# The end of a decode step of two attention and two gated blocks: head 5 with V held still, heads 6 and 7 past the row sum, x laid in rows ahead of them, and a last norm that takes both sums at once

## Chip, cores, metric

One of the eight cores of a Trainium2 chip. The metric is the device time of one execution in microseconds (us). Lower is better. TensorE is PE (its weight loads PEld), VectorE DVE, ScalarE ACT, GpSimd POOL, SyncE SP.

## What is computed

Four tokens (B = 4, one position each, D = 512) go through attention, a gated block, attention and a gated block again, with the same weights and the same cache both times:

```python
x = A_x
x = x + _A_ref(_layernorm(x), A_k_cache, A_v_cache, A_wq, A_wo)
x = x + _B_ref(_layernorm(x), B_w_gate, B_w_up, B_w_down)
x = x + _A_ref(_layernorm(x), A_k_cache, A_v_cache, A_wq, A_wo)
x = x + _B_ref(_layernorm(x), B_w_gate, B_w_up, B_w_down)

# _A_ref: 32 query heads on 8 key/value heads, the last 2048 positions of the cache
p = softmax((x @ wq) @ k^T * 128 ** -0.5);  return (p @ v) @ wo
# _B_ref: F = 1792
return (sigmoid(x @ w_gate) * (x @ w_up)) @ w_down
# _layernorm: (x - mean) / sqrt(var + 1e-5)
```

## The kernel before

Every step is an operation with an engine, a guessed duration, what it reads and writes and a priority (`_Plan.op`, L55). `_schedule` (L96) simulates the engines with these durations and writes down one order for each engine, in which the chip then runs it; a wait is put ahead of an operation for what it reads, for what it overwrites, and for a PSUM bank that another engine used before (`banks`). SP's operations are DMA issues, kept in the order of the program. An engine takes its operations strictly in that order, so an operation that waits holds all that stand behind it.

The first attention (L = 0) and the first gated block (glu 1) are not touched by the change, but for guessed durations. The second attention (L = 2) finds all of K transposed in SBUF (`kt`), so only V is streamed: head by head (`HEADS2`, 0 to 7) into places of `WHERE["V2_h"]`; from head 2 on into the part of `kt` whose head has had its scores. Head 5 has one transfer of 2 MB, head 6 two halves, head 7 one of 1 MB, one of 640 KB and a piece of 384 KB kept from the first attention. Behind V come w_gate, w_up (half of each is kept) and w_down in four pieces for the last gated block.

For a head h (n-th in order; here n = h) of the second attention:

- `scores` (L750): 16 matmuls (L759) into PSUM bank 3 or 0, the maximum on DVE (smax L768, sadd L772, strn L774, smin L778), the exponential on ACT (L781), its transpose on DVE (ptr, L787), and PT, two matmuls (L792);
- `weights` (L804): the probabilities are spread over the four tokens by DVE (ptx, L817) and ACT (pta, L824, four instructions); the row sum zb (L832) and its reciprocal rz (L836). These are the softmax's row sums;
- `pv_wo` (L874): probabilities times V. For heads 2 to 5 (`WIDE[2]`) the probabilities are held still and V moves (`wide_pv`, L852, 32 matmuls of 256 columns); ACT copies the result (L860), and PVs adds its parts up with two float32 matmuls (L867). For the others V is held still (L895, 64 matmuls of 32 columns, in order of the pieces) and nothing is left to add. Then omul (L906, times the reciprocal), a selection by four matmuls (sel, L932), osel (L939), and WO, four matmuls of 512 columns into bank 7 (`WB`, L947), which keeps a sum over heads 0 to 6 (`NWR = 7`) in rows. Head 7 goes past that sum: sixteen matmuls of four columns with wo held still (L917), and the result is added to x directly.

`early_residual(2)` (L954) is planned ahead of head 7: it takes the row sum of bank 7 as a high and a low half (w_hi on ACT, L960, with a load of the sigmoid's table; w_lo on DVE, L966), turns it by eight matmuls (w_turn, L973) and adds it to x (L979).

The last gated block (`glu(3, True)`, L1033) begins with `layer_norm(3)` (L575): xn = x in bfloat16 (L560), x itself (L563), x split into three bfloat16 parts (L583, L585, L586, and x_1 on POOL, L1018), the sum over D by three matmuls (L591) and a reduce (L597), center (L606), square (L618), reduce (L621), a second sum (L579), the variance (L626) and the power -1/2 on POOL (rstd, L630). Beside it the gate and up matmuls run on x not yet normalized (L1050, 112 of four columns), and the mean's part is taken off later (L569, L1066 gc and uc) and rstd multiplied in (L1066 gm and sr). The sigmoid is on ACT (L1071), the product h on DVE (L1090). `x_rows` (L1017) lays x as rows into bank 2 by twelve matmuls (L1026), on which w_down (L1119, 56 matmuls) adds up, so that one copy (L1132) and one DMA write the result.

Of the kernel before, what the change touches and what calls it, by code (L numbers as in the profile page):

```python
# [268 lines left out]
def build(nc, A_x, A_k, A_v, A_wq, A_wo, B_wg, B_wu, B_wd, out):  # L269
# [35 lines left out]
    AHEAD = 2  # L305
    NWR = 7
    WIDE = {0: {0: 4, 1: 4, 2: 4, 3: 4, 4: 4, 5: 4, 6: 2}, 2: {2: 2, 3: 2, 4: 2, 5: 2}}
    VKEEP = {0: 24, 7: 26}
# [30 lines left out]
    with es:  # L339
# [6 lines left out]
        side = nc.alloc_sbuf_tensor_at("side", [128, NS * UNIT], BF16, offset=SIDE)  # L346
        csum = nc.alloc_sbuf_tensor_at("csum", [128, HQ + 2 * NFC], F32, offset=SCRATCH)
        cs_q, cs_g, cs_u = csum[:, 0:HQ], csum[:, HQ:HQ + NFC], csum[:, HQ + NFC:HQ + 2 * NFC]
        ident_r = sb("ident_r", [128, 4 * 128], BF16)
        ident_b = ident_r[:, 0:128]  # L350
# [16 lines left out]
        eye32 = pt[:, 256:288]  # L367
        small = pt[:, 0:1024]
        perm = sb("perm", [128, 128], BF16)
        ofb, ofr = (lambda t: (t[:, 0:NB], t[:, NB:2 * NB]))(sb("ofbr", [128, 2 * NB], F32))  # L370
# [74 lines left out]
        })  # L445
        for h in range(2, HKV - 2):
            WHERE["V2_%d" % h] = [("kt", (h - 2) * UHEAD, UHEAD)]

        def bankb(b):
# [116 lines left out]
        def means(L, out, cs, n):  # L566

            P.op("vector", "mean%d_%d" % (L, n), c_dve(n * NB),
                 lambda v: v.scalar_tensor_tensor(  # L569
                     out[:, :].rearrange("p (f b) -> p f b", b=NB), lr1[:, :].unsqueeze(1).broadcast_to([128, n, NB]),  # L570
                     1.0 / D, cs.unsqueeze(2).broadcast_to([128, n, NB]), ALU.mult, ALU.mult),
                 r=[("pss",), ("cs",)], w=[("mc", id(out))])
            return ("mc", id(out))

        def layer_norm(L, factor=1.0):  # L575
# [5 lines left out]
            if late:  # L581
# [7 lines left out]
                def e_xsum(t):  # L589
                    for i, part in enumerate([by2(xnv)] + x_at[L][1:]):  # L590
# [6 lines left out]
                     lambda v: v.tensor_reduce(lr1[:, :], ps[:, MB, 0:NX].rearrange("p (c b) -> p b c", c=NC), AXX, ALU.add),  # L597
                     r=[("psx",)], w=[("pss",)], banks=(MB,))
            else:
                P.op("vector", "ln_r1_%d" % L, c_dve(NX),  # L600
# [238 lines left out]
        def wide_pv(L, n, h, wide, bank, out, s):  # L839
# [24 lines left out]
            def e_sum(pe):  # L864
                last = None
                for c in range(wide):
# [5 lines left out]
                 w=[("pso", out[0], 0)], banks=(out[0],))  # L872

        def pv_wo(L, n, h, pbk, pieces, prev=()):  # L874
            k2 = n % 2
            kp, ptv, pk = pt_of(L, n)
            wide = WIDE[L].get(n, 0)
            obk = (3 if n == HKV - 1 else pbk[k2]) if L else 6 if wide else 5
            p0 = 0 if L == 0 else 256
# [4 lines left out]
            for s, j0 in () if wide else pieces:  # L884
                def e_pv(pe, s=s, j0=j0):
                    last = None
                    j1 = j0 + s[2] * UNIT // 128
                    for j in range(j0, j1):
# [14 lines left out]
            ov = onb[:, k2 * NR:(k2 + 1) * NR]  # L903
            r0 = p0 if wide else NR
            P.op("vector", "omul%d_%d" % (L, h), c_dve(NR),
                 lambda v: v.tensor_tensor(ov.rearrange("p (r b) -> p b r", r=REP),  # L906
                                           ps[:, obk, r0:r0 + NR].rearrange("p (b r) -> p b r", b=NB),
                                           rz[:, kp * NR:(kp + 1) * NR].rearrange("p (b r) -> p b r", b=NB), ALU.mult),
                 r=[("pso", obk, j0) for _, j0 in pieces] + [("rz", kp)], w=[("on", k2)], banks=(obk,))

            o0 = p0 + 4 * NR if wide else 4 * NR
            if n >= NWR:
                def e_wo(pe):
                    last = None
                    for c in range(NC):
                        for r_ in range(REP):
                            last = pe.matmul(ps[:, obk, o0 + c * NB:o0 + (c + 1) * NB],  # L917
                                             dcol(wo_sb, c, h * WOH + r_ * D),
                                             ov[:, r_ * NB:(r_ + 1) * NB],
                                             start=(c == 0 and r_ == 0), stop=(r_ == REP - 1), skip_group_check=True)  # L920
                    return last
                P.op("tensor", "WO%d_%d" % (L, h), tm["pe_pair"] * NC * REP, e_wo,
                     r=[("wo", h), ("on", k2)], w=[("psl", obk)], banks=(obk,))
                residual("w_acc%d_%d" % (L, h), ps[:, obk, o0:o0 + NX], [("psl", obk)], obk, L == 2 and n == HKV - 1)
                return
# [3 lines left out]
            def e_sel(pe):  # L929
                last = None  # L930
                for j in range(4):
# [9 lines left out]
                                           ofr[:, :].unsqueeze(1).unsqueeze(3).broadcast_to([128, 4, REP, NB]), ALU.mult),  # L941
                 r=[("psl", obk), ("ofr",)], w=[("onr",)], banks=(obk,))

            def e_wo(pe):
                last = None
                for j in range(4):
                    last = pe.matmul(ps[32 * j:32 * j + NR, WB, 0:D], onr[:, j * NR:(j + 1) * NR],  # L947
                                     wo_sb[:, h * WOH + j * D:h * WOH + (j + 1) * D],
                                     start=(n == 0), stop=(n == NWR - 1), skip_group_check=True)
                return last  # L950
# [3 lines left out]
        def early_residual(L):  # L954


            hi, lo = pb[:, 0:D], pb[:, D:2 * D]
            tk = [("psw", n) for n in range(NWR)]
            def e_hi(a):
# [21 lines left out]

        GB, UB, YB = 0, 1, 2
        STASH = ((8, 3), (12, 0), (16, 1), (20, 2))
# [32 lines left out]

        def x_rows():  # L1017
            P.op("gpsimd", "x_1", 300.0, lambda g: g.tensor_copy(x_at[3][0], by2(xnv)), r=[("xn",), ("xz",)], w=[("x1",)])  # L1018

            def e_x(pe):  # L1020
                last = None
                for part in range(3):
                    for i in range(2):
                        for half in range(2):
                            a0 = 32 * (1 - half) + 2 * part + i
                            last = pe.matmul(ps[:, YB, i:128:2], xz[:, a0:a0 + 128], ident_b[:, 64 * half:64 * half + 64],  # L1026
                                             start=(part + i + half == 0), stop=False, skip_group_check=True)
                return last
            P.op("tensor", "x_rows", 12 * tm["pe_pair"], e_x, r=[("x1",), ("x2",), ("x3",), ("ident_b",)],
                 w=[("psyx",)], banks=(YB,), prio=len(P.ops) + 400)  # L1030
            return [("psyx",)]

        def glu(L, last_layer):  # L1033
            GB, UB, YB = (0, 1, 2) if last_layer else (QB, QB + 1, MB)
            layer_norm(L)
            prev = []
            toks = {"g": [], "u": []}
            xin = x_rows() if last_layer else []
            wid = NB if last_layer else NB + 1
            for nm, ktc in (("u", 0), ("u", 1), ("g", 0), ("g", 1), ("g", 2), ("g", 3), ("u", 2), ("u", 3)):  # L1040
# [4 lines left out]
                def e_g(pe, ktc=ktc, s=s, bank=bank):  # L1045
                    last = None
                    for fc in range(NFC):
# [7 lines left out]
                    return last  # L1055
                prev = [P.op("tensor", "glu_%s%d_%d" % (nm, L, ktc), tm["pe_pair"] * NFC, e_g,
                             r=list(blk_tok(s)) + [("xn",)], w=[("psg", bank, ktc)], banks=(bank,), order=prev)]
                toks[nm].append(("psg", bank, ktc))
            NH_ = NFC * NB

# [14 lines left out]
            if last_layer:  # L1075
                mg, mu = means(L, tg, cs_g, NFC), means(L, tu, cs_u, NFC)
                mul("glu_gc", tg, fb(pg), fb(tg), toks["g"] + [mg], mg, (GB,), ALU.subtract)
                mul("glu_gm", gm, fb(tg), rs3, [mg, ("rstd",)], ("gm",))
                P.op("scalar", "glu_sig%d" % L, c_act(NH_), e_sig, r=[("gm",)], w=[("sg",)])
                mul("glu_sr", sg, fb(sg), rs3, [("sg",), ("rstd",)], ("sg",))  # L1080
                mul("glu_uc", um, fb(pu), fb(tu), toks["u"] + [mu], ("um",), (UB,), ALU.subtract)
            else:
                mul("glu_gm", gm, fb(pg), rs3, toks["g"] + [("rstd",)], ("gm",), (GB,))
# [45 lines left out]
            if not last_layer:  # L1129
                residual("glu_res%d" % L, ps[:, YB, 0:NX], ytoks, YB, True)  # L1130
                return
            P.op("vector", "out_cp", c_dve(128), lambda v: v.tensor_copy(pb[:, 0:128], ps[:, YB, 0:128]),  # L1132
                 r=ytoks, w=[("pb", 0)], banks=(YB,))
            dma("out", out_d.rearrange("b (c d) -> c b d", c=NC), pb[0:128:8, 0:128], w=[("out_dram",)], r=[("pb", 0)],
# [27 lines left out]
        def load_wo(h):  # L1162
            to = wo_sb[:, h * WOH:(h + 1) * WOH]
            if h >= NWR:
                dma("wo_%d" % h, to.rearrange("p (r n) -> p r n", r=REP), wo_d[:, h * REP:(h + 1) * REP, :],
                    w=[("wo", h)], rate="bw_1k")
            else:
                dma("wo_%d" % h, to, A_wo[h * REP * 128:(h + 1) * REP * 128, :].rearrange("(p j) n -> p (j n)", j=4),
                    w=[("wo", h)])
# [55 lines left out]
        def v2_head(n):  # L1225
            h = HEADS2[n]
            if n == min(WIDE[2], default=-1):
                eyes(2, sx(20, 1), sorted(set(WIDE[2].values())))
            if n == NWR:
                early_residual(2)  # L1230
            pv_wo(2, n, h, (5, 6), vs2[h], turns[n + 1:n + 2])

# [74 lines left out]
```

## Time and profile before

| what | us |
|---|---|
| median of 3 runs | 175.23 (175.01 to 175.37) |
| the profiled execution | 176.48 |
| its span, first to last instruction | 174.6 (174.64) |
| PE busy | 139.6 (80%) |
| DVE busy | 99.5 (57%) |
| ACT busy | 75.4 (43%) |
| POOL busy | 6.8 (4%) |
| read from HBM | 69.08 MB, 396 GB/s over the span |

The profiled execution is 1.25 us longer than the median; 1.84 us of it lie outside of the span. In the page, a slice is one fortieth of the span (4.37 us), a digit the busy share in tenths, and PEclk the granted clock of TensorE. In the chain of waits each row is a start, a duration and what the end waited for in that stretch: an engine with a tile and a line, a transfer, or "issue" where the profile shows no wait. In the timeline a row is start, duration, engine, line, operation and shapes, and in brackets the idle time ahead of it and what ended that. A matmul's "start to start" is the distance of two such starts in one group; a transfer's landing is its issue plus the time to landing that the trace gives.

### The profile page before, as it was taken

Reading aid. Unit: us, or ns where it says so; the run is one execution under the profiler, and the core shown is the slowest. Engines: PE = TensorE matmul, PEld = TensorE weight load, DVE = VectorE, ACT = ScalarE, POOL = GpSimd, SP = SyncE. Lnnn points to the kernel's source line nnn. Section 1 sums busy time; section 2 is a strip of 40 time slices with the busy share of each in tenths; the row PEclk is TensorE's granted clock in tenths of the full one; section 3 lists DMA queues with packets and bytes.
Section 4 is the critical chain, followed back from the end, with each engine's and each line's share of the span. In section 5 each row is a group of like instructions: output and inputs, shape, how many; then the busy total and the mean of one; then the engine's idle time right before and its main releaser. Section 6 shows DMA issues by size and latency. Waiting matters only on the chain.

```text
span 174.6 us, 4868 instructions
## 1 busy us (share of the span) xinstructions
PE 139.6 (80%) x2175; PEld 102.3 (59%) x2175; DVE 99.5 (57%) x246; ACT 75.4 (43%) x129; POOL 6.8 (4%) x17
## 2 busy tenths in 40 slices
PE   0395589899899679998969776548887999798794
PEld 0293488657566468564745466547424765576693
DVE  7435015886858484795897733014267988842440
ACT  2064216748476636566391240304424654730300
POOL 5200000000000000000000000100100000000020
PEclk9999755999999987999999755555555999955555
DMA  5999999999999999999999999999999999999940
GB/s 181 420 444 408 420 439 424 428 411 443 428 415 426 406 438 424 410 451 409 439 422 401 390 417 416 409 402 394 410 427 436 433 420 418 417 412 424 407 171 5
DMA packets 9504, 69.39 MB, mean 397 GB/s; under 512 B 1032, under 2 KB 2188, under 8 KB 6156
## 3 DMA queue, kind: packets, MB, share of 16 engines
q1 hardware_dynamic: 9476, 69.08, 95.3%
q8 instruction: 17, 0.28, 0.6%
q14 instruction: 3, 0.02, 0.0%
q10 hardware_dynamic: 8, 0.00, 0.0%
HBM read 69.08 MB, written 0.00 MB: 396 GB/s over the span
## 4 chain that ended last, share of the span: by engine, by line
DMA 54%; PE 33%; DVE 5%; ACT 4%; SPq 1%; issue 1%; DVEq 0%; ACTq 0%
DMA arena<-in_A_v_cache_dram 31%; DMA kt<-in_A_k_cache_dram 12%; PE ps L852 7%; PE ps L759 7%; DMA wo_sb<-in_B_w_gate_dram 6%; DMA wo_sb<-in_A_wq_dram 5%; PE ps L736 4%; PE ps L1050 3%; PE ps L895 3%; PE ps L867 2%; SPq L461 1%; PE ps L832 1%; PE ps L947 1%; ACT pb L781 1%; ACT pt L824 1%
## 5 line engine op out<-in xcount | busy, mean ns | idle before, releaser
L746 ACT COPY kt<-ps 128x1024 bf16<-128x1024 bf16 x40 | 39.3, 1016 | 28.9 <-PE ps L736 28.6
L736 PE MATMUL ps<-ident_r,kt 128*128 128x128 bf16 x512 | 40.6, 240 | 5.4 <-DMA kt<-in_A_k_cache_dram 3.2
L736 PEld LDWEIGHTS ps<-ident_r,kt 128*128 128x128 bf16 x512 | 35.3, 111 | 12.1 <-issue 4.0
L746 DVE COPY kt<-ps 128x1024 bf16<-128x1024 bf16 x24 | 29.1, 1214 | 15.1 <-PE ps L736 14.9
L759 PE MATMUL ps<-kt,qs 128*32 128x512 bf16 x256 | 20.4, 448 | 1.3 <-DVE qs L715 0.7
L817 DVE TENSOR_TENSOR pt<-ps,ofbr 128x1024 bf16<-128x1024 f32 (+1 forms) x15 | 15.4, 1030 | 2.7 <-PE ps L792 2.6
L852 PE MATMUL ps<-arena,pt 128*64 128x512 bf16 (+1 forms) x128 | 12.7, 361 | 3.1 <-DMA arena<-in_A_v_cache_dram 3.1
L768 DVE TENSOR_REDUCE nmz<-ps 128x1 f32<-128x512 f32 x16 | 11.0, 687 | 6.8 <-PE ps L759 6.5
L781 ACT ACTIVATE pb<-ps,nmz 128x512 bf16<-128x512 f32 x16 | 11.1, 695 | 5.7 <-DVE nmz L778 5.7
L787 DVE STREAM_TRANSPOSE pb<-pb 128x512 bf16<-128x512 bf16 x16 | 11.2, 702 | 3.8 <-ACT pb L781 3.8
L824 ACT ACTIVATE pt<-ps,ofbr 128x96 bf16<-128x96 f32 x28 | 7.2, 342 | 10.6 <-PE ps L792 10.6
L759 PEld LDWEIGHTS ps<-kt,qs 128*32 128x32 bf16 x256 | 5.9, 105 | 8.3 <-issue 2.6
L852 PEld LDWEIGHTS ps<-arena,pt 128*64 128x64 bf16 (+1 forms) x128 | 5.7, 106 | 7.9 <-DMA arena<-in_A_v_cache_dram 4.0
L832 PE MATMUL ps<-rowf,nmz 128*128 128x16 f32 x32 | 7.3, 304 | 2.3 <-DVE pt L817 2.2
L860 ACT COPY arena<-ps 128x512 f32<-128x512 f32 (+1 forms) x7 | 3.9, 555 | 11.6 <-PE ps L852 11.5
L832 PEld LDWEIGHTS ps<-rowf,nmz 128*128 128x128 f32 x32 | 5.7, 225 | 5.2 <-DVE pt L817 3.5
L630 POOL TENSOR_TENSOR rs<-pt,rs 128x4 f32<-128x4 f32 x4 | 4.1, 1013 | 119.8 <-DVE pt L626 119.8
L867 PEld LDWEIGHTS ps<-arena 128*128 128x128 f32 x52 | 6.7, 201 | 2.1 <-ACT arena L860 1.6
L867 PE MATMUL ps<-arena 128*128 128x16 f32 x52 | 7.4, 273 | 0.7
L1050 PE MATMUL ps<-xn,arena 128*128 128x5 bf16 (+1 forms) x168 | 6.3, 172 | 2.0 <-DMA arena<-in_B_w_up_dram 1.1
L1050 PEld LDWEIGHTS ps<-xn,arena 128*128 128x128 bf16 x168 | 6.3, 118 | 2.2 <-DMA arena<-in_B_w_up_dram 1.2
L947 PE MATMUL ps<-wo_sb,onr 128*16 128x512 bf16 x56 | 6.4, 442 | 1.4 <-DVE onr L939 1.4
(143 smaller groups left out, 158.0 us busy)
## 6 DMA issues: line engine op xcount, KB each, us to landing
kt<-in_A_k_cache_dram SPq DMA_DIRECT2D x8, 2048.0 KB, 24.8
arena<-in_A_v_cache_dram SPq DMA_DIRECT2D x7, 2048.0 KB, 20.1
kt<-in_A_v_cache_dram SPq DMA_DIRECT2D x4, 2048.0 KB, 15.6
wo_sb<-in_A_wo_dram SPq DMA_DIRECT2D x8, 512.0 KB, 25.4
kt<-in_A_v_cache_dram SPq DMA_DIRECT2D x3, 1024.0 KB, 17.0
kt<-in_A_wq_dram SPq DMA_DIRECT2D x1, 2048.0 KB, 11.8
side<-in_A_wq_dram SPq DMA_DIRECT2D x1, 1984.0 KB, 15.9
arena<-in_B_w_up_dram SPq DMA_DIRECT2D x2, 896.0 KB, 8.4
```

Of the source, the lines that this page charges most:

```text
L736: last = pe.transpose(bankb(bank)[:, (v * NB + q) * 128:(v * NB + q + 1) * 128], kt[:, c0:c0 + 128], ident_b[:, :])
L746: return (e.tensor_copy if ev == "vector" else e.copy)(to, fr)
L759: last = pe.matmul(ps[32 * b:32 * b + 32, sbk, 0:CB * 128], qs[:, q0:q0 + 32], blk_ap(kblk(h, b))[:, c * CB * 128:(c + 1) * CB * 128], sta ...
L768: lambda v: v.tensor_reduce(nmv, ps[:, sbk, 0:CB * 128], AXX, ALU.max, negate=True),
L781: o = a.activation(pbuf[:, :], ps[:, sbk, 0:CB * 128], ACTF.Exp, bias=gv, scale=1.0, accum_out=zv)
L787: P.op("vector", "ptr%d_%d" % (L, h), 650.0, lambda v: v.transpose(turned[:, :], pbuf[:, :]), r=[("pb", 0), ("pb", 1)], w=[("pb", 2), ("pb ...
L817: lambda v: v.tensor_tensor(pv4[:, 0:nj], spread(tbk, nj).unsqueeze(2).broadcast_to([128, nj, NB, REP]), ofb[:, :].unsqueeze(1).unsqueeze( ...
L824: last = a.mul(pv4[:, nj:NJ4, b, :], spread(MB, NJ4 - nj), ofb[:, b:b + 1])
L832: lambda pe: pe.matmul(ps[:, tbk, CB * NQ:CB * NQ + NR], zv.broadcast_to([128, 128]), rowf[:, :], start=True, stop=True),
L852: last = pe.matmul(ps[rows * g:rows * (g + 1), bank, 0:wide * 128].rearrange("p (c d) -> p c d", c=wide), ptv[:, w0:w0 + rows], v, start=( ...
L867: last = pe.matmul(ps[:, out[0], out[1]:out[1] + NR], part[:, c * 128:(c + 1) * 128], ey[wide][:, c * NR:(c + 1) * NR], start=(c == 0), st ...
L1050: last = pe.matmul(ps[:, bank, fc * wid:(fc + 1) * wid], cols[:, fc - g0, :], xn[:, ktc * (NB + 1):ktc * (NB + 1) + wid], start=(ktc == 0 ...
```

## The change

- V of head 5 comes in two halves into the same place, and head 5 leaves `WIDE[2]`: V is held still, 64 matmuls of 32 columns.
- `NWR` is by layer: the row sum of the second attention holds heads 0 to 5. Heads 6 and 7 go past it (`wo_last`): wo held still, into bank 5, where the two add up. Head 6 still takes sel and osel, for its wo is laid out for them, and then `oc`, a reduce over the selections.
- `early_residual(2)` is planned ahead of head 6. Its row sum, and later the wo products of heads 6 and 7, are also added as rows to the result (`early_shift`, `wo_rows`; WOr_e, WOr_6, WOr_7, 25x128 matmuls).
- `x_rows` becomes `early_rows`, planned ahead of head 6, with x as it was before the second attention: three groups of four matmuls, and its four steps (x_1, x_rest, x_2, x_3) on POOL. The result's bank YB is 3 instead of 2.
- The last norm (`last_norm`) sums x minus the mean that x had before the second attention (kept by POOL's `s_keep`, taken off by `x_s`) and its square in one reduce and one float32 matmul; variance and mean come out of both sums by five small DVE steps. rstd is multiplied into gate and into up (gm, ur), and no longer into the sigmoid's result.
- gate/up matmuls are planned with 36 ns instead of 29, which moved nothing outside of the end.

```diff
-    NWR = 7
-    WIDE = {0: {0: 4, 1: 4, 2: 4, 3: 4, 4: 4, 5: 4, 6: 2}, 2: {2: 2, 3: 2, 4: 2, 5: 2}}
+    NWR = {0: HKV - 1, 2: HKV - 2}
+    WIDE = {0: {0: 4, 1: 4, 2: 4, 3: 4, 4: 4, 5: 4, 6: 2}, 2: {2: 2, 3: 2, 4: 2}}
...
+        WHERE["V2_%d" % (HKV - 3)] = [("kt", 3 * UHEAD, UHEAD // 2), ("kt", 3 * UHEAD + UHEAD // 2, UHEAD // 2)]
...
+                P.op("gpsimd", "s_keep", 300.0, lambda g: g.tensor_copy(sD, lr1[:, :]), r=[("pss",)], w=[("sD",)])
...
+        GB, UB, YB = 0, 1, 3
+        XB, X0 = 5, 128
+        xsrc = ps[:, XB, X0:X0 + NX]
...
+        def wo_last(n, h):
+            o_ = oc(n)
+
+            def e_wo(pe):
+                last = None
+                for c in range(NC):
+                    for j in range(REP):
+                        last = pe.matmul(ps[:, XB, X0 + c * NB:X0 + (c + 1) * NB], dcol(wo_sb, c, h * WOH + j * D),
+                                         o_[:, j:j + 25:8], start=(n == NWR[2] and c == 0 and j == 0),
+                                         stop=(n == HKV - 1 and j == REP - 1), skip_group_check=True)
+                return last
+
+            P.op("tensor", "WO2_%d" % h, 600.0, e_wo, r=[("wo", h), ("oc", n)], w=[("psl", XB, n)], banks=(XB,))
+            if n < HKV - 1:
+                wo_rows(n, h)
+
+        def wo_rows(n, h, behind=()):
+            o_ = oc(n)
+
+            def e_rows(pe):
+                last = None
+                for j in range(REP):
+                    for c in range(NC):
+                        w0 = h * WOH + j * D + c * 128
+                        last = pe.matmul(ps[32 * c:32 * c + 25, YB, 0:128], o_[:, j:j + 25], wo_sb[:, w0:w0 + 128],
+                                         start=False, stop=False, skip_group_check=True)
+                return last
+            P.op("tensor", "WOr_%d" % h, 600.0, e_rows, r=[("wo", h), ("oc", n), ("psyx",)], w=[("psyr", n)], banks=(YB,),
+                 prio=len(P.ops) + 400, order=behind)
...
+            tail = L == 2 and n >= NWR[2]
+            final = tail and n == HKV - 1
+            to = oc(n).rearrange("p (b y) -> p b y", y=8)[:, :, 0:REP] if final else ov.rearrange("p (r b) -> p b r", r=REP)
...
+            if tail:
+                def e_oc(v):
+                    with nc.allow_low_precision("three of four are zero"):
+                        return v.tensor_reduce(oc(n).rearrange("p (b y) -> p y b", y=8)[:, 0:4],
+                                               onr[:, :].rearrange("p (j r b) -> p j b r", r=REP, b=NB), AXX, ALU.add)
+                P.op("vector", "oc%d_%d" % (L, h), c_dve(4 * NR), e_oc, r=[("onr",), ("xz",)], w=[("oc", n)])
+                wo_last(n, h)
+                return
...
-        def x_rows():
-            P.op("gpsimd", "x_1", 300.0, lambda g: g.tensor_copy(x_at[3][0], by2(xnv)), r=[("xn",), ("xz",)], w=[("x1",)])
...
+        def early_shift():
+
+            P.op("vector", "x_s", c_dve(NX),
+                 lambda v: v.scalar_tensor_tensor(
+                     xs.rearrange("p (c b) -> p c b", c=NC), sD.unsqueeze(1).broadcast_to([128, NC, NB]), -1.0 / D,
+                     xT[:, :].rearrange("p (c b) -> p c b", c=NC), ALU.mult, ALU.add),
+                 r=[("sD",), ("xT",)], w=[("tin",)])
...
+            P.op("tensor", "WOr_e", 320.0, e_h, r=[("pb", u) for u in range(4)] + [("o8",), ("psyx",)], w=[("psyr", 0)], banks=(YB,),
+                 prio=len(P.ops) + 100)
+
+        def early_rows():
+
+            xf, rest = (a.rearrange("p (k i b) -> p k i b", k=2, i=2) for a in (xT[:, :], xr3))
+            x1, x2, x3 = x_at[3]
+            P.op("gpsimd", "x_1", 300.0, lambda g: g.tensor_copy(x1, xf), r=[("xT",), ("xz",)], w=[("x1",)])
+            P.op("gpsimd", "x_rest", 300.0, lambda g: g.tensor_tensor(rest, xf, x1, ALU.subtract), r=[("xT",), ("x1",)],
+                 w=[("xr3",)])
+            P.op("gpsimd", "x_2", 300.0, lambda g: g.tensor_copy(x2, rest), r=[("xr3",), ("xz",)], w=[("x2",)])
+            P.op("gpsimd", "x_3", 300.0, lambda g: g.tensor_tensor(x3, rest, x2, ALU.subtract), r=[("xr3",), ("x2",)], w=[("x3",)])
+            for part in range(3):
...
+                P.op("tensor", "x_rows%d" % part, 480.0, e_x, r=[("x1",), ("x2",), ("x3",), ("ident_b",)] + [("psyx",)] * (part > 0),
+                     w=[("psyx",)], banks=(YB,))
+
+        def last_norm():
...
+            P.op("vector", "xb_last", c_dve(NX), lambda v: v.tensor_tensor(xnv, c4(xsrc), c4(xT[:, :]), ALU.add),
+                 r=toks + [("xT",)], w=[("xn",)], banks=(XB,))
+            P.op("vector", "ln_center3", c_dve(NX), lambda v: v.tensor_tensor(xc[:, :], xsrc, xs, ALU.add),
+                 r=toks + [("tin",)], w=[("xc",)], banks=(XB,))
...
+            P.op("vector", "ln_r12_3", c_dve(2 * NX), lambda v: v.tensor_reduce(part, both, AXX, ALU.add),
+                 r=[("xc",), ("sq",)], w=[("lr2",)])
+            P.op("tensor", "ln_sum3", tm["pe_f32"],
...
+            P.op("vector", "ln_m1", c_dve(NB), lambda v: v.tensor_copy(lr1[:, :], s1), r=[("psv",)], w=[("lr1",)], banks=(MB,))
+            P.op("vector", "ln_m2", c_dve(NB), lambda v: v.scalar_tensor_tensor(m2, lr1[:, :], -1.0 / D, s1, ALU.mult, ALU.mult),
+                 r=[("psv",), ("lr1",)], w=[("lr2",)], banks=(MB,))
+            P.op("vector", "ln_v3", c_dve(NB), lambda v: v.tensor_tensor(m2, s2, m2, ALU.add),
+                 r=[("psv",), ("lr2",)], w=[("lr2",)], banks=(MB,))
...
+            if last_layer:
+                wo_rows(HKV - 1, HEADS2[-1], prev)
...
+                P.op("vector", "glu_ur%d" % L, c_dve(NH_),
+                     lambda v: v.scalar_tensor_tensor(fb(um), fb(um), root, rs3, ALU.mult, ALU.mult),
+                     r=[("um",), ("rstd",)], w=[("um",)])
...
-            if n == NWR:
+            if n == NWR[2]:
+                early_rows()
                 early_residual(2)
+                early_shift()
```

The order that the planner writes for PE around the change, behind the row sum that starts at 150.41 before: x_rows (first four), PT 6, sum of head 4, first half of V5, selection 4, row sum 6, second half of V5, WO 4, PT 7, selection 5, x_rows (eight more), WO 5, row sum 7, first half of V6, kept piece of V7, w_turn, second half of V6, WOr_e, selection 6, wo of head 6, first part of V7, WOr 6, the rest of V7, wo of head 7, 28 gate/up matmuls, ln_sum, 84 gate/up matmuls, WOr 7, w_down.

## Prediction

> **What bounds the kernel now.** I read the granted clock and slices of the page first, then the chain of waits from the second attention on, then the timeline of each engine after 146 us, the landing of each transfer, and the DMA share in short windows near the end.
>
> The page says that DMA is busy to the 38th slice, and that the TensorE clock in the tail is half:
>
> ```profile
> PEclk9999755999999987999999755555555999955555
> DMA  5999999999999999999999999999999999999940
> ```
>
> Windows of 0.5 us (PE, PEld, DVE, ACT, POOL busy, clock, DMA share, GB/s) give the end of the stream: the last weights (quarter four of w_down) are issued at 149.92 and land 20.1 us later, at 170.0.
>
> ```profile
> 168.50:169.00 0.50, 0.50 (x20) 0.50 (x18) 0.00 (x0) 0.00 (x0) 0.49 (x1) 0.50 0.34 131
> 169.00:169.50 0.50, 0.50 (x9) 0.50 (x7) 0.22 (x1) 0.23 (x1) 0.00 (x0) 0.50 0.09 33
> 169.50:170.00 0.50, 0.50 (x8) 0.50 (x6) 0.41 (x3) 0.02 (x1) 0.00 (x0) 0.50 0.00 0
> ```
>
> But the end doesn't wait for it. The chain of waits (start, us, what):
>
> ```profile
> 153.16 1.73 PE ps L852 x32
> 154.89 0.02 issue
> 154.91 0.38 ACT side L860
> 155.29 0.04 issue
> 155.34 1.03 PE ps L867 x4
> ...
> 161.17 0.59 ACT pb L960
> 161.76 0.02 issue
> 161.79 0.70 DVE pb L966
> 162.49 0.14 issue
> 162.62 0.35 PE ps L973 x8
> ...
> 164.45 0.19 DVE xn L560
> ...
> 169.06 1.31 PE ps L1026 x12
> 170.37 0.09 issue
> 170.46 1.71 PE ps L1119 x56
> ```
>
> From 148 us on no link is a transfer. V of head 5 lands at 152.35 and is multiplied at 152.99; the halves of head 6 land at 154.83 and 157.31 and start at 156.21 and 158.58; the pieces of head 7 land at 159.80 and 161.38 and start at 161.05 and 162.84. PE and the hand-offs run 0.6 to 1.5 us late, and after x (164.63) come 5.84 us up to the first w_down matmul (170.46). So there is something to win, but not beyond the stream: a bound for later.
>
> **The unit costs**, start to start, from the timeline's rows at half clock: a V-still matmul (L895) 27 ns (25 at full clock), a WO of four (L947) 0.54 us until the next group starts, a selection (L932) 0.14, the row sum (L832) 0.43, PT (L792) 0.21, sixteen wo matmuls of four columns (L917) 0.45 and 0.17 for the last one's result, an x_rows matmul (L1026) 107 ns, a w_down matmul of 25x128 (L1119) 25 ns. Hand-offs between engines are 0.04 to 0.06 us, DVE's small operations 0.16 to 0.23.
>
> **Up to 150.7 us nothing moves.** PE's order is the same up to the row sum at 150.41. The copy s_keep stands on POOL while it waits for the variance (12 us idle before 121.90): nothing. Without that cover it would delay rstd by its 0.27.
>
> **V of head 5 in two halves.** Half-sized pieces took 2.48 us each (154.83 to 157.31), a whole V 4.90 (147.45 to 152.35): 0.06 later for all that follows, so the last landing becomes 170.05. The extra issue (0.54 us on SP) stands in a queue whose transfers land 16 to 22 us after issue: nothing. The first half now lands at 149.93. Removed: the wide product, ACT's copy (0.37), the sum (1.03). Added: 64 x 25 to 27 ns.
>
> **x in rows early.** Twelve matmuls leave the path between gate/up and w_down; four go behind the row sum of 150.41 (full clock, 0.2 us), eight behind selection 5 (8 x 107 = 0.86). The first four add a wait on POOL's x_1, x_rest, x_2, x_3, one behind the other from 148.74 (end of the memset). PE needs them at 150.73, and everything of PE is queued behind: PT of head 6, and through it ptx, pta and the exponential of head 7. So the chain has 2.0 us, 0.50 a step. The rows of POOL:
>
> ```profile
> 148.50 0.24 POOL L1242 MEMSET qs<- 128x168 bf16 x1 [25.59 <-PE ps L759]
> 164.77 0.27 POOL L1018 COPY qs<-xn 128x16 bf16<-128x16 bf16 x1 [16.02 <-DVE xn L560]
> 167.99 1.01 POOL L630 TENSOR_TENSOR rs<-pt,rs 128x4 f32<-128x4 f32 x1 [2.95 <-DVE pt L626]
> ```
>
> The copies are 0.27. The two subtractions have no row: below stands POOL's shortest, a memset of two columns at 0.10, above the power, also a TENSOR_TENSOR, at 1.01. I take 0.3, since shape and kind of work are the copy's: done by 150.2, no wait. At 1.01 for the subtractions the chain ends at 151.6 and PE stands 0.9. [...]
>
> **The walk on PE.** x_rows 150.73 to 150.93. PT 6 waits for the transpose (151.06), 151.12 to 151.25. Sum of head 4 to 151.72, result 151.87. DVE: ptx 6 151.44 to 152.25, omul 4 to 152.36, smin 7 to 152.46 (it was 151.66); exponential 7 at 152.49 instead of 152.35, transposed at 154.03. PE: first half of V5 151.75 to 152.55, selection 4, row sum 6 to 153.02, second half (landed 152.42) 153.03 to 153.89, WO 4 to 154.52, PT 7 to 154.73, selection 5 to 154.87, x_rows to 155.73. ptx 7 now stands ahead of osel 5 on DVE (154.95 to 155.77), osel 5 to 155.91, so WO 5 starts at 155.97: 0.24 of idle PE. Row sum 7 to 156.93, V6a to 157.79, kept V7 to 158.11. w_hi (0.59) and w_lo (0.70) follow WO 5's end (156.57) and are done at 157.91, beside this: **the 1.45 us gap of L960 and L966 (161.17 to 162.62) goes.** w_turn to 158.32, V6b to 159.18, WOr_e (8 x 25 ns and 0.1 of switching) beside omul 6, selection 6 to 159.78. Then osel and, new, oc (reduce of 64, 0.22): result 160.46, wo at 160.52 to 160.97, in order ahead of V7a, so 0.74 of idle PE instead of 0.32. V7a to 161.83, WOr 6 0.5, V7b 162.42 to 162.95, omul 163.33, wo 163.39, result 163.98, **x at 164.20, against 164.63: 0.43 earlier.** On PE between: out go the sum 1.03 with its wait and the gap of w_turn; in come x_rows 1.06, WOr 0.7, oc 0.22.
>
> **The last norm.** From x on: center, square, the reduce of both in 0.54; ln_sum behind the first 28 gate/up matmuls (165.18), result 165.75; four small DVE steps to 166.57, power 166.65 to 167.66. Before: eight DVE steps and two sums, rstd at 168.99. Gone are x_rest, x_2, x_3, their sum and its reduce. So rstd is no longer last: g is ready at 167.57, gc 167.82, gm 168.07, sigmoid 168.35. What is late next is u: gate/up is 112 x 32.5 ns and ln_sum 0.43, end 168.48 (it was 169.06); uc 168.73, ur 168.98, h 169.28. WOr 7 (0.5) lies on PE beside uc to h: nothing. w_down starts at 169.33 against 170.46, **1.13 us earlier.** Its last eight would start at 170.52, behind their landing (170.05).
>
> **The sum.** 174.64 - 1.13 = 173.5 of span; 1.84 lies around it (176.48 - 174.64), so 175.35 for such an execution. The median shown is 1.25 below the profiled one; taken off it, 175.23 - 1.13 = 174.1.
>
> **Rivals.**
>
> *Full clock for longer (17%).* The granted clock changes in steps of 3.41 us here: it is full from 135.96 to 153.03, half before and after. The stretch 149.62 to 153.03, after which it fell, had 2.60 us of PE in 35 matmuls; the change puts 32 V-still and four x_rows matmuls more into it. The Trainium skill, TensorE: Matmul & The Clock Gate, "Part 1: The HAM clock gate (the "warmup" mystery)", says that activity in free-running windows of 3413 ns grants the clock; by that rule one busier window buys the next. The lengths here (3.413, 17.067, 34.133) agree. With it, the second stretch shrinks by half of WO, PT, row sum and x_rows, some 0.7 us. Then the stream binds: last landing 170.05, eight matmuls 0.5, copy 0.33: end of copy at 170.92, not 172.48, so 1.56 at most: 173.7. Against it: the stretch 60.87 to 64.28 held 35 matmuls too, half of them of 128 columns on the full array, about as much array work as I count for the new stretch, and the clock fell behind it all the same (64.28).
>
> *POOL's subtractions at 1.01 (12%).* 0.9 of standing PE, all on the path since V lies ready: 0.2 to 0.3 gained, 174.9.
>
> *Many small gaps (7%).* Each switch between kinds of matmul costs up to 0.1 more than my unit costs (157.95 to 158.04 shows 0.09): some eight more switches on the path, 0.7 lost, 174.8.
>
> *Slower: POOL's chain blocks PE (9%).* PE takes its work in order, and x_rows stands ahead of all the rest. If each of the four steps takes the power's 1.01 and a hand-off, the chain ends at 153.1: 2.4 of standing PE, 0.2 won back at WO 5: 176.2. It costs from 2.0 us of chain on and turns the sign from about 3.1. For it: the same opcode; and at the start a DVE copy of 128x16 took 1.13 us beside POOL's 0.97 memset, so the two can hold each other. Against: 0.27 for the copies.
>
> That the change is not in effect is excluded: its order moves the rows named.
>
> **Chances.** Forecast 55%, 173.9 to 174.5 by itself. About 0.2% (0.35 us) can be told from no change. Faster by more: 0.55 + 0.17 and half of the two small rivals, 0.81; within 0.10; slower 0.09. The range goes from the stream's bound less a little, 173.5, to 175.1, past the small rivals.
>
> **What would show it.** Right: PE's first x_rows at 150.7 to 150.9; L960 at about 156.6; x between 164.0 and 164.4; ln_sum directly behind 28 gate/up matmuls; rstd before u; first w_down matmul at 169.3, no wait on a landing. Wrong: a wait of PE on POOL before x_rows; V5's second half later than 153.5; idle PE of over 1 us ahead of head 6's wo; a w_down matmul that waits for DMA (then the clock or the small steps did better than I say).

## The result: 0.7% slower, by holes that no step of the prediction contains

| what | before | after |
|---|---|---|
| median beside each other on the same chip, us | 175.46 (174.80 to 177.15, 22 runs) | 177.01 (175.32 to 178.05, 22 runs) |
| ratio of after to before (of the means, after's longest run left out) | | 1.0066, interval 1.0039 to 1.0093 |
| the profiled execution and its span, us | 176.48, 174.64 | 178.05, 176.31 |
| matmuls recorded on TensorE | 2175 | 2252 |
| x ready; first w_down matmul, us | 164.63; 170.46 | 165.95; 172.13 |

Both profiled executions are long ones, 1.02 and 1.04 us above the medians in this table (the one of after is the longest of its 22), so their difference, 1.57, is that of the medians, 1.55. First the two rows of slices of the page of after, granted clock and DMA:

```profile
PEclk9999756999999999999999655555556999995555
DMA  5999999999999999999999999999999999999920
```

The clock stayed full for longer (135.64 to 159.53; before it fell at 153.03): the first rival's condition came true, and the time went up all the same. The chain of waits of after (start, us, what) says where it went:

```profile
160.11 0.59 PE ps L893 x16
160.70 0.63 PE ps L937 x23
161.33 1.94 issue
163.27 0.40 PE ps L937 x9
...
165.76 0.19 DVE xn L1121
...
167.50 1.19 PE ps L1170 x37
168.69 0.78 issue
169.47 1.66 PE ps L1170 x47
...
172.13 1.70 PE ps L1245 x56
```

Head 6's wo matmuls (L893) start at 160.11, 0.41 ahead of the prediction's walk on PE. Then TensorE stands for 1.94 us in the middle of 32 like matmuls of V (L937), behind the 23rd, and for 0.78 us in the middle of the gate/up (L1170), behind the 65th of 112. Such a stand is called a hole here. "issue" means that the profile shows nothing that was waited for: V7's two pieces had landed at 159.67 and 161.25, and the last gate/up weights at 165.57, ahead of their use. A third such hole, 0.12, lies at 156.75. The three add up to 2.84 us, and 172.13 less 2.84 is 169.29: the walk had 169.33.

**What the holes are.** The page of either kernel lists among its DMA queues (packets, MB, share of 16 engines):

```profile
q8 instruction: 17, 0.28, 0.6%
```

In the packet records each of the 17 has 16384 bytes. The DMA view of after can be cut to the two stretches ahead of and within the large hole. From 156.9 to 160.6 us it lists one queue:

```profile
q1 hardware_dynamic: 271, 1.54, 101.2%
```

From 160.6 to 161.9 it lists a code packet besides:

```profile
q8 instruction: 1, 0.02, 5.3%
```

So the data queue q1 fills all 16 engines and no code moves for 3.7 us; then one packet does, and TensorE goes on at 163.27, 1.46 us behind the packet's end. Now count the matmuls that TensorE executed. The holes of after stand ahead of matmuls 1878, 2005 and 2133 of its records: 127 and 128 apart, and a few records can be missing. Each matmul has a weight load, so one hole is 256 instructions from the next. Such a place, the start of a block of 256, is called a border here. The packets' starts and ends, set beside the times at which TensorE passes these borders, from the records of both traces:

| kernel | passes a border | next code packet | passes the next border | standing there |
|---|---|---|---|---|
| before | 142.50 | 147.26 to 148.36 | 149.76 | 0.25 |
| before | 149.76 | 153.53 to 154.61 | 158.70 | 0 |
| before | 158.70 | 161.28 to 162.29 | 165.19 | 0 |
| before | 165.19 | 166.98 to 167.98 | 170.74 | 0 |
| after | 149.61 | 154.50 to 155.60 | 156.87 | 0.12 |
| after | 156.87 | 160.70 to 161.81 | 163.27 | 1.94 |
| after | 163.27 | 166.93 to 168.02 | 169.47 | 0.78 |

So the theory, called F: TensorE's code comes in blocks of 256 instructions, 128 matmuls with their weight loads. The packet for the next block starts only after TensorE has entered the present one, and beside a full stream of data it starts 1.8 to 4.9 us later (at the end, where the stream is over, 1.1 to 1.6). It takes 1.0 to 1.1 us and, where TensorE stood waiting, is of use 1.3 to 1.5 us after its end. By this theory a block isn't passed in less than the sum, however short its matmuls are. Before passed its last blocks in 8.94, 6.49 and 5.55 us; the packet had landed 4.09, 2.90 and 2.76 us ahead of the next border, so at least 1.2 us were to spare. After has 77 matmuls more behind 150.7 us, 154 instructions, and its clock was full for 6.5 us longer, so its borders come sooner: 7.26, 6.40, 6.20 us, each time at the limit.

The Trainium skill, Runtime: NRT & Kernel Launch, "Instruction fetch mechanics", describes this queue: blocks of 16 KiB or 256 instructions, the next one fetched while the present one runs, at a cost "mostly hidden". The block size agrees with the 16384 bytes of a packet; the hiding doesn't hold here: 1.94 us stood open.

### The profile page after: what moved, and what is told of

It is laid out like the page before. It is cut to its first block, busy times and chain, and to the rows that moved or that the text cites. A ratio compares the mean times of both kernels' runs of the same rounds, so it can differ in the third digit from the quotient of the medians.

```text
span 176.3 us, 5028 instructions
## 1 busy us (share of the span) xinstructions
PE 137.0 (78%) x2252; PEld 100.4 (57%) x2252; DVE 99.5 (56%) x247; ACT 75.1 (43%) x128; POOL 7.8 (4%) x22
## 4 chain that ended last, share of the span: by engine, by line
DMA 53%; PE 28%; DVE 8%; ACT 4%; issue 3%; SPq 1%; DVEq 0%; ACTq 0%
DMA arena<-in_A_v_cache_dram 31%; DMA kt<-in_A_k_cache_dram 12%; PE ps L764 6%; DMA wo_sb<-in_B_w_gate_dram 6%; PE ps L857 5%; DMA wo_sb<-in_A_wq_dram 5%; PE ps L741 4%; PE ps L937 3%; PE ps L1170 3%; ACT pb L786 2%; DVE pb L792 2%; DVE nmz L773 2%; SPq L464 1%; ACT pt L829 1%; PE ps L797 1%
## 5 line engine op out<-in xcount | busy, mean ns | idle before, releaser
L741 PE MATMUL ps<-ident_r,kt 128*128 128x128 bf16 x512 | 39.6, 235 | 5.7 <-DMA kt<-in_A_k_cache_dram 3.4
L741 PEld LDWEIGHTS ps<-ident_r,kt 128*128 128x128 bf16 x512 | 33.9, 107 | 12.5 <-issue 4.0
L1193 ACT ACTIVATE pt<-pt 128x56 f32<-128x56 f32 x2 | 0.5, 250 | 20.4 <-DVE pt L1202 12.7
L837 PE MATMUL ps<-rowf,nmz 128*128 128x16 f32 x32 | 6.7, 285 | 2.4 <-DVE pt L822 2.2
L1170 PE MATMUL ps<-xn,arena 128*128 128x5 bf16 (+1 forms) x168 | 6.3, 172 | 2.8 <-DMA arena<-in_B_w_up_dram 1.1
L837 PEld LDWEIGHTS ps<-rowf,nmz 128*128 128x128 f32 x32 | 5.2, 203 | 5.2 <-DVE pt L822 3.8
L1170 PEld LDWEIGHTS ps<-xn,arena 128*128 128x128 bf16 x168 | 6.3, 118 | 3.0 <-issue 1.5
L635 POOL TENSOR_TENSOR rs<-pt,rs 128x4 f32<-128x4 f32 x3 | 3.0, 1015 | 106.1 <-DVE pt L631 106.1
```

The source lines that it names most:

```text
L741: last = pe.transpose(bankb(bank)[:, (v * NB + q) * 128:(v * NB + q + 1) * 128], kt[:, c0:c0 + 128], ident_b[:, :])
L837: lambda pe: pe.matmul(ps[:, tbk, CB * NQ:CB * NQ + NR], zv.broadcast_to([128, 128]), rowf[:, :], start=True, stop=True),
L1170: last = pe.matmul(ps[:, bank, fc * wid:(fc + 1) * wid], cols[:, fc - g0, :], xn[:, ktc * (NB + 1):ktc * (NB + 1) + wid], start=(ktc == 0 ...
```

## The experiments

In the texts on record F is this theory; the rivals are described in each. All ratios are to the kernel before on the same chip. Its medians there were 175.75, 175.78, 175.60 and 176.20 us, with single runs from 174.4 to 177.4.

**1. The changed kernel with a light stream.** Edit (the same for the gate/up and w_down weights of the last layer):

```
-                dma("V%d_%d_%d" % (L, h, u0), blk_ap(s), v_d[h][:, :, u0 * UNIT:(u0 + n) * UNIT], w=blk_tok(s),
+                few = 32 if L == 2 and h >= 6 else n * UNIT
+                dma("V%d_%d_%d" % (L, h, u0), blk_ap(s)[:, 0:few], v_d[h][:, :, u0 * UNIT:u0 * UNIT + few], w=blk_tok(s),
```

> The changed kernel with the same order on every engine, but the transfers of V of heads 6 and 7 and of the last gated block's weights cut to 32 columns each (most of these data are left out, so the result is not the reference's). Theory F (instruction supply): PE's code comes in blocks of 256 instructions (16 KB) over the DMA engines; a block is asked for when PE enters the one before it, and behind a full data stream it is usable only 6 to 7 us later. PE's three gaps inside groups of like matmuls (0.12 us at 156.75, 1.94 at 161.33, 0.78 at 168.69) are waits for blocks. With the stream gone from about 152 us on, blocks come in under 5 us, the gaps go, w_down starts at about 169.3 instead of 172.13: 174.2 us, 1.6% under the changed kernel. Rival C (the gaps belong to TensorE's clock, which fell at 159.53): they stay, 177.0. Rival V (late V or weights): gaps at 161.33 go, since V lies ready; this run alone doesn't tell V from F, the padded kernel does.

Measured: 173.75 us (173.56 to 174.12, four runs), ratio 0.989 (0.9835 to 0.9946). The same groups in its chain of waits, V7 and gate/up:

```profile
160.03 0.81 PE ps L938 x32
...
164.49 2.72 PE ps L1173 x84
...
168.21 1.70 PE ps L1248 x55
```

All 32 and all 84 run through without a hole. The code packets start 0.2 to 0.7 us after a border from 155.97 on, and the same matmuls in the same order reach w_down at 168.21, where 169.3 was expected; the clock stayed full to 160.99. So the work that the change adds isn't what costs.

**2. The kernel before with the same light stream.** The same edit.

> The kernel before with the same cut of the stream (most of the data of V 6, V 7 and the last weights left out). Theory F: its only gap inside a group (0.25 us at 149.52) lies before the stream ends, its other blocks came in time: 175.2 to 175.5, no change that can be told. Rival V: also no change, since no link of its chain after 148 us is a transfer. A gain of 1 us or more would speak against both: then the stream slows something else.

Measured: 176.20 us (174.00 to 177.27), ratio 0.9969 (0.9916 to 1.0022); w_down starts at 169.92. A lighter stream gives before nothing that can be told, so experiment 1 isn't a general gain from less data. Beside the same light stream the changed kernel has the lower median, 173.75 for 176.20; the executions of before scatter over 3.3 us, so how much of this is the change stays open.

**3. The kernel before with its borders moved.** Edit:

```
+        def e_pad(pe):
+            for _ in range(24):
+                last = pe.matmul(ps[:, 0, 0:4], ident_b[:, :], ident_b[:, 0:4], start=True, stop=True, skip_group_check=True)
+            return last
+        P.op("tensor", "pad", 700.0, e_pad, r=[("ident_b",)], banks=(0,))
```

> The kernel before with 24 small matmuls added at its start, where PE idles until 4 us. Theory F: they shift all block borders by 48 instructions; the border that stood behind w_down's first matmuls now stands ten matmuls before the end of x_rows, and its block, asked for at about 164, is usable only about 1 us after PE needs it: a gap inside x_rows at about 169.1, w_down 0.6 to 1.0 later, 176.1 us (+0.4%). Rivals C and V, and any theory in which the change's own work costs the time: 24 matmuls in idle time cost nothing, 175.4.

Measured: 175.83 us (175.47 to 176.34), ratio 1.0009 (0.9979 to 1.0038). The chain of waits shows the hole in x_rows (L1032), where none was before:

```profile
167.59 0.34 PE ps L1032 x3
167.94 0.28 issue
168.22 1.12 PE ps L1032 x9
```

The place is F's, the size isn't (0.28): in this execution the clock stayed full to 158.53 and the addition that gives x started at 163.00 instead of 164.45, so the time shows no loss. Another hole, 0.48 us, ended at 141.07 inside wide V matmuls; it stands 510 recorded matmuls ahead of the one in x_rows, four blocks but for two records. The chain doesn't pass through it, for up to 157.15 it follows a transfer. This run supports F by the place alone.

**4. The changed kernel with head 5 wide again**, 56 instructions fewer (`WIDE` and `WHERE` of head 5 as before).

> The changed kernel with head 5 as before (one transfer, V moves, ACT's copy and the sum): 28 matmuls, 56 instructions fewer on PE in the end. Theory F: the borders stand 56 instructions later in the work; w_down starts at about 171.2 instead of 172.1: 176.1 us. Theory H (V-still of head 5 is itself the loss): 175.4 or less. Theory N (head 5 has no part in it): 177.0, or slower by the 0.4 us of the sum.

Measured: 176.53 us (176.01 to 177.47), ratio 1.0041 (1.0005 to 1.0077). The holes moved on and shrank (chain of waits):

```profile
162.89 0.17 PE ps L936 x3
163.06 0.98 issue
...
167.30 2.10 PE ps L1169 x65
169.40 0.30 issue
```

With 28 matmuls fewer ahead of them, both holes stand 28 matmuls later: the first behind 9 more of V7, the 16 of WOr_6 and 3 of V7's second piece, the second behind the 93rd of the gate/up (28 and these 65) instead of the 65th. w_down starts at 171.46 (171.2 by F). The time alone doesn't decide, for 176.53 lies between F's 176.1 and theory N's 177.0; the places do. Theory H falls with the time.

**5. The changed kernel with its borders moved by 160 instructions** (experiment 3's edit with 80 matmuls).

> The changed kernel with 80 small matmuls more at its start, where TensorE waits for the first loads; nothing else is touched. Theory F (instruction supply): every later block border moves back by 160 instructions, so the holes leave the places where they were (behind the 23rd of V7's first 32 matmuls, behind the 65th of the gate/up) and come to two others: about the 3rd matmul of V6's second half (0.5 to 0.9 us, at about 160) and about the 2nd matmul of head 7's wo (about 1.0 us, at about 166). The blocks still take 6.2 to 6.5 us each, so little is won or lost: 176.3 to 177.8 us. Theory W (the holes belong to those groups of matmuls, their data or their slots): they stay behind the 23rd and the 65th, 177.0 us.

Measured: 177.66 us (175.69 to 178.50), ratio 1.0088 (1.0051 to 1.0126). In the chain of waits head 7's wo (L899) and its row product (L916):

```profile
164.24 0.27 PE ps L899 x4
164.50 1.22 issue
165.72 0.50 PE ps L899 x12
...
170.92 1.00 issue
```

V7 and the gate/up now run through; the hole stands behind the 4th of head 7's wo matmuls, where F had put it within two matmuls, and the groups' theory W falls. Two points were missed: V6 got no hole, and one came in WOr_7, 128 matmuls behind the other, where I had thought the stream over.

**6. The changed kernel without the two parts that add the most matmuls** (56 of the 77): head 5 wide, head 6 in the row sum.

```
-    NWR = {0: HKV - 1, 2: HKV - 2}
+    NWR = {0: HKV - 1, 2: HKV - 1}
```

> The changed kernel with head 5 wide and head 6 inside the row sum, as before: what is left of the change is x in rows ahead, head 7's row product and the last norm with both sums at once. It has 42 instructions more on TensorE in its last 25 us than the kernel before, where the change has 154. Theory F: the block borders fall on about the 13th of head 7's 16 wo matmuls and on the end of the gate/up; holes of 0 to 0.5 and of 0.3 to 1.0 us, w_down from 170.2 to 171.2, 174.7 to 175.9 us in all. Theory W (the row products and the x moved ahead are what costs, by their own time on TensorE): the hole inside V7 is still over 1 us and w_down starts later than 171.5, 176.5 us.

Measured: 175.46 us (174.70 to 176.39), ratio 1.0002 (0.9972 to 1.0031): before's time. One hole in the tail is left, 0.46 us in WOr_7, nine matmuls behind the end of the gate/up where F had one, and w_down starts at 170.58. There is none in head 7's wo, where F allowed 0 to 0.5. The row products of head 7 and x in rows are still there, so theory W falls.

**7. The same with its borders moved by 208 instructions** (104 matmuls at the start).

> The kernel of e6 with 104 small matmuls more at its start, by which its block borders move back by 208 instructions. Theory F: they come to about the 17th matmul of V6's second half and to the first third of the gate/up, over 6.5 us apart, and the next one behind the end of the stream; no hole over 0.4 us behind 150 us, w_down from 169.8 to 170.6, 174.2 to 175.2 us: below the kernel before. Theory W: more work at the start can't make the end earlier; as e6 or slower.

Measured: 176.68 us (175.81 to 177.47), ratio 1.0043 (1.0011 to 1.0074). The holes went as F said: one behind 150 us, 0.32 at 170.27 inside w_down, which started at 169.53. The time did not: 174.2 to 175.2 was expected, and it went up as theory W had it. The padding came ahead of x, and the last weights landed at 172.08, where experiment 6 has 169.97. Experiment 9 takes the first of these two away.

**8. Head 5's part of the change alone**, in the kernel before.

```
-    WIDE = {...  2: {2: 2, 3: 2, 4: 2, 5: 2}}
+    WIDE = {...  2: {2: 2, 3: 2, 4: 2}}
```

> The kernel before with one part of the change alone: head 5 holds V still (56 instructions more ahead of about 155 us). Theory F: the borders fall on the first half of V6 and on the 3rd of head 7's wo matmuls, about 7 us apart, so no hole over 0.3 us behind 150 us; 174.8 to 175.9 us. Theory W (holding head 5's V still costs in itself): 176.0 us or more, V5's second half later than 153.5.

Measured: 175.34 us (174.92 to 175.94), ratio 0.9978 (0.9950 to 1.0007). No hole over 0.2 us behind 150, w_down at 169.00 in the profiled run. Its 28 additional matmuls lie where the blocks have room, and cost nothing that can be told: it isn't the number of instructions alone, but how many fall into the time of one fetch.

**9. Experiment 7 with the padding where TensorE is idle.**

```
+        P.op("tensor", "pad_a", 700.0, e_pad, r=[("ident_b",)], banks=(0,), order=[xt_op])
...
+                P.op("tensor", "pad_b", 700.0, e_pad, r=[("ident_b",)], banks=(0,), order=[lv_op])
```

> The kernel of e7 with its 104 small matmuls put in two parts where TensorE stands idle (52 behind the transposes of x, 52 behind the first norm's second sum), so that nothing at the start comes later: e7's 104 took 2.93 us ahead of x and moved its whole stream about 1 us later. Theory F (instruction supply): the same block borders as e7, so no hole over 0.4 us behind 150 us; with the stream back in its place w_down starts at 169.8 to 170.4, 174.2 to 175.3 us in all, level with the kernel before or a little below. If instead the borders' place in itself makes the last weights late (in e7 one of 16 DMA engines ended 2.1 us behind the others), the last landing is again about 172 and the time 176.5.

Measured: 176.91 us (175.81 to 177.48), ratio 1.0069 (1.0037 to 1.0100). The expectation's second case came true. w_down started at 169.65, ahead of before's 170.46, and then waited for its weights (timeline of TensorE; idle time and its end in brackets):

```profile
170.40 0.82 PE L1252 MATMUL ps<-kt,pt 128*25 128x128 bf16 x16
171.65 0.61 PE L1252 MATMUL ps<-kt,pt 128*25 128x128 bf16 x16 [0.42 <-DMA kt<-in_B_w_down_dram]
```

The last weights landed at 172.22 instead of experiment 6's 169.97, as in experiments 5 (172.49) and 7 (172.08). The packet records show that from 170.6 to 171.8 a single data packet at a time was under way, one behind the other, as from one of the 16 DMA engines. A code packet had run from 168.06 to 169.16, but whether on that engine they don't say, and one such packet (1.1 us) would not be the whole lag. Why the last weights come late stays open, and no version that beats the kernel before beyond doubt was found.

**10. The supply by itself**: the kernel before with 560 small matmuls at the start and 640 behind w_down.

> The supply measured by itself: the kernel before with 560 small matmuls at its start, where the stream of loads runs, and 640 at its end, behind the last transfer of weights. 104 such matmuls took 2.93 us in e7, 28 ns each, so 128 of them (256 instructions with their weight loads, one block) need 3.6 us. Theory F: at the start a block takes 5.5 to 7 us while the DMA engines are full, with holes of 2 to 3 us between runs of 128 matmuls; at the end, with the DMA engines idle, 3.6 to 4.2 us, with holes under 0.6 us. Theory W (no limit of supply): 3.6 us for 128 matmuls in both places.

Measured, in one execution: 199.36 us; the page lists 26 code packets for 3375 matmuls, where before has 17 for 2175. The timeline of TensorE at the start, beside a full stream, and at the end, beside none:

```profile
2.00 6.11 PE L547 MATMUL ps<-ident_r 128*128 128x4 bf16 x223 [2.00 <-POOL xn L494]
10.10 3.55 PE L547 MATMUL ps<-ident_r 128*128 128x4 bf16 x128 [2.00 <-issue]
16.29 3.56 PE L547 MATMUL ps<-ident_r 128*128 128x4 bf16 x128 [2.65 <-issue]
23.58 2.30 PE L547 MATMUL ps<-ident_r 128*128 128x4 bf16 x81 [3.74 <-issue]
...
179.99 14.68 PE L1140 MATMUL ps<-ident_r 128*128 128x4 bf16 x551
194.81 2.53 PE L1140 MATMUL ps<-ident_r 128*128 128x4 bf16 x89 [0.15 <-issue]
```

At the start TensorE stops for 2.00, 2.65 and 3.74 us, with exactly 128 matmuls between the stops; the first row's 223 are 95 up to a border that it passes without a stop, at 4.55, and one block of 128. The blocks take 5.55, 6.19 and 7.29 us. At the end 128 of them take 3.2 to 3.7 us without a hole over 0.3. The windows view (4.5 to 25 us and 180 to 197 us) shows a DMA share of 1.00 and of 0.02. VectorE, ScalarE and GpSimd stand all but idle in both, and within a run the matmuls come 27 to 28 ns apart at both ends. The difference that the trace shows is the stream.

**11. The changed kernel with smaller data packets.**

```
+                cut = [(0, n)]
+                if L == 2 and h in (5, 6, 7):
+                    cut = [(0, n // 2), (n // 2, n - n // 2)]
```

> The changed kernel with each transfer of V of heads 5, 6 and 7 cut into two of half the columns, so that its packets are half as large; all bytes and all matmuls stay. It asks what holds the code packet back, which starts 3.7 to 4.9 us after a border here. If it waits behind a fixed number of data packets, the waits at 150 and 157 fall to about 2 us, the hole in V7 goes and w_down starts about 170: 175 us. If the wait doesn't follow the packets' size (in the changed kernel it was 2.4 to 3.5 us in stretches of 16384-byte packets and 2.0 to 4.9 in stretches of 4096 to 8192), the holes stay as they are: 176.5 to 177.5 us. I take the second.

Measured: 178.48 us (177.68 to 179.46), ratio 1.0135 (1.0090 to 1.0181). The code packets start 5.58, 3.21 and 4.00 us after their borders, and the holes are there (chain of waits):

```profile
161.06 1.17 issue
...
167.62 1.21 issue
```

The second case, which was taken, came true for the holes; the time is 1 us above its 176.5 to 177.5. A fixed number of data packets ahead of the code isn't the rule. What sets the wait of 2 to 5 us stays open. Why this kernel is slower than the changed one stays open too; its clock fell earlier, at 151.36.

## Why the prediction was wrong, point by point

- **What bounds the kernel now.** Right as read, but not complete. It says that from 148 us on no link of the chain is a transfer; the row `149.52 0.25 issue`, inside 32 wide V matmuls of before, is one: the border at 149.76, 0.25 us of code that was late. I took it for nothing. In the chain of before:

```profile
148.75 0.76 PE ps L852 x23
149.52 0.25 issue
149.77 0.50 PE ps L852 x9
```

- **Up to 150.7 us; head 5 in halves; x in rows early.** Right. PE's first x_rows came at 150.85 (150.7 to 150.9 was forecast), V5's halves at 152.02 and 153.18 (151.75 and 153.03). POOL's two subtractions, bounded by 0.10 and 1.01 and taken at 0.3, are these rows of its timeline:

```profile
149.52 0.23 POOL L1101 TENSOR_TENSOR qs<-xT,qs 128x16 f32<-128x16 f32 x1
150.14 0.27 POOL L1104 TENSOR_TENSOR qs<-qs 128x16 bf16<-128x16 f32 x1
```

  The same opcode at 1.01 is the power. The rival "POOL's subtractions at 1.01" and the slower one, "POOL's chain blocks PE", thereby fall: there was no wait of PE on POOL.
- **The walk on PE.** The step that failed. Its order, its groups and its hand-offs came as written up to head 6's wo (160.52 said, 160.11 measured, with 0.58 of idle ahead of it for 0.74; the clock stayed full to 159.53, where the walk has it half from 153.03). But it lets a matmul start as soon as its data and the one before it allow, 25 to 27 ns apart, and takes for granted that TensorE has the instruction. "V7a to 161.83" ended at 163.67 instead: 1.94 us of missing code. x came at 165.95, not 164.20.
- **The last norm.** The order is right: ln_sum stands directly behind the first 28 gate/up matmuls, and rstd is ready ahead of u. The size is off by two terms. From x to w_down are 6.18 us, where the walk has 5.13: 0.78 is the second hole, and 0.27 are small gaps (in experiment 1, without the hole, the stretch is 5.25, 0.12 over the walk). For the gate/up and ln_sum the walk has 4.23 us (164.25 to 168.48), and experiment 1 has 4.20; the terms that it gives for them, 112 x 32.5 ns and 0.43, add up to 4.07 only.
- **The sum.** The 1.13 us that it hoped for are in the work: less its 2.84 us of holes, after would reach w_down at 169.29. That this meets the walk's 169.33 within 0.04 is luck: without its holes after would have x at 163.89, 0.31 ahead of the walk and with a full clock that the walk didn't have, and lose 0.27 again in the last norm. Experiment 1 ran at 173.75, near the 174.1 that was forecast; it also has a stretch of full clock to 160.99, so the agreement isn't one of every term.
- **The rivals.** "Full clock for longer" happened, and its 173.7 did not: the matmuls came to the border sooner, and waited there. "Many small gaps" put 0.7 us; from x to w_down experiment 1 shows 0.12. None of the rivals had the instructions as a resource. "The stream binds" came true in another way in experiments 7 and 9.
- **The chances.** 0.09 for slower was too low for a change that puts 77 more matmuls into the last 25 us. The sign hung on a resource that could have been read: 17 packets of a queue named "instruction", and one hole in the chain of before.

## What to carry to other kernels

A row "issue" in the middle of a group of like matmuls is not noise: compare it with the packets of the instruction queue, and count the instructions since the last such hole. Where TensorE stood beside full DMA engines, a block of 128 matmuls with its loads had taken 5.5 to 7.3 us, so a run of matmuls at 25 to 33 ns (3.2 to 4.2 us a block) can last one block and then stand. The count says where a hole can come, not how long it is, for the wait of the code packet varies. Before wide matmuls are traded for many narrow ones ahead of the end of a stream, count the blocks; short work that fits a block's spare time is free, as experiment 8 shows, and the same work beyond it is paid in holes.

## What the runs showed of the hardware

- Code for TensorE arrived in packets of 16 KB that serve 128 matmuls with their weight loads; the hole falls on one matmul, whatever group it belongs to (experiments 3, 4, 5 and 10; 17 packets for 2175 matmuls, 26 for 3375).
- The code packet starts 1.8 to 5.6 us after a border beside a full stream and at most 1.6 us after it beside little or none (experiments 1, 2 and 10, and the ends of the other kernels); it follows no simple rule of packet size (experiment 11).
- In the three kernels whose borders were moved by 160 or 208 instructions (experiments 5, 7 and 9) the last weights landed at 172.1 to 172.5 instead of 169.9 to 170.0, with the start in place too (experiment 9). The cause wasn't settled.
